# Natural row order for the first four token tiles of a fused layer-norm, linear-attention and gated-MLP kernel

## The chip, the cores and the metric

The kernel runs on one core of one Trainium2 chip. Times are device microseconds (us) of that core; a shorter time is better. Before the change the median of the first three runs was 213.92 us (213.84 to 214.03). Runs of one kernel usually agree within 0.3%.

## The reference, cut to what matters

```python
xn = layernorm(x)                       # x: 2048 tokens x 512, bf16
qkv = xn @ wqkv                         # 32 heads of 16
# feature maps softmax(+-q w_phi), softmax(+-k w_phi); linear attention; @ wo
# gated MLP: ((xn @ w_gate) * (xn @ w_up)) @ w_down, inner width 1792
out = x + attention(xn) + mlp(xn)
```

Every token is treated alike. Which token sits in which partition of which tile is free, as long as loads, residual loads and stores agree.

## The kernel before

The 2048 tokens are 16 tiles of 128 (partition x 512 features). One helper maps a tile to rows of DRAM, for the loads of `x`, for the second (residual) loads of `x` and for the stores:

```python
def rows(ap, t0, n):
    g, r = divmod(t0, 4)
    return ap[g * 512:(g + 1) * 512, :].rearrange("(p r) d -> p r d", r=4)[:, r:r + n, :]
```

So tile 0 holds rows 0, 4, 8, ... of the first 512. A row is 1 KB, and the rows of one tile lie 4 KB apart. Tiles 0 and 1 are loaded in halves of 256 columns, from two queues, so that the layer norm can start early:

```python
for t in range(2):
    load_x_half(t, 0, SP)      # 64 KB: 128 pieces of 512 B
    load_x_half(t, 1, ACT)
load_x(2, 1)                   # 128 KB: 128 rows of 1 KB
load_v(ACT, 1)                 # v weights, 128 KB each
load_v(SP, 0)
load_v(ACT, 3)
load_v(SP, 2)
load_x(3, 1)
load_gu(SP, 0, (0,))           # first gate weights
load_gu(SP, 0, (1,))           # first up weights
...
```

The head of the compute, in an order that is fixed on each engine:

```python
warm(7)                          # matmuls of 512 columns on constants
warm(1, 512, [("x", 0)])         # one more when tile 0 is there
ln_mean_split(0)                 # half the mean on VectorE, half on ScalarE
ln_mean_split(1)
ln_center_split(0)               # VectorE
ln_center_split(1)
x_transpose(0, 2, 0)             # TensorE, then ScalarE copies from PSUM
ln_mean_split(2)                 # waits for tile 2
x_transpose(0, 3, 1)
warm(1, 128)
x_transpose(1, 4, 0, DVE)        # copied from PSUM by VectorE, behind tile 2's mean
ln_center_whole(2)
x_transpose(1, 5, 1, DVE)
warm(1, 128)
... # v matmuls of tiles 0 and 1 (weights 1, 0), tile 2's transposes, v matmuls (3, 2), ...
... # v of tile 2, first gate half, tile 3's transposes, first up half, ...
```

Of the kernel before, what the change touches and what calls it, by code (L numbers as in the profile page):

```python
# [125 lines left out]
def _build(nc, es, A_x, A_wqkv, A_w_phi, A_wo, B_w_gate, B_w_up, B_w_down, out):  # L126
# [137 lines left out]

    def rows(ap, t0, n):
        g, r = divmod(t0, 4)
        return ap[g * 512:(g + 1) * 512, :].rearrange("(p r) d -> p r d", r=4)[:, r:r + n, :]

    def load_x(t0, n, eng=SP):
        o = sb("x", t0 * 512, n * 512).rearrange("p (t d) -> p t d", t=n)  # L270
        i = rows(x_flat, t0, n)
        sc.dma(eng, lambda e: e.dma_start(o, i), [], [("x", t) for t in range(t0, t0 + n)], n * 131072)

    def load_x_half(t, h, eng):
        c = slice(h * 256, h * 256 + 256)
        o, i = x_tile(t)[:, c], rows(x_flat, t, 1)[:, 0, c]
        sc.dma(eng, lambda e: e.dma_start(o, i), [], [("x", t) if h else ("x", t, 0)], 65536)  # L277
# [4 lines left out]
    def load_residual(t0):  # L282
        o = sb("xr", (t0 % 4) * 512, 1024).rearrange("p (t d) -> p t d", t=2)
        i = rows(x_flat, t0, 2)
        over = [("ek", 2 + t0 // 2, h) for h in range(2)] if t0 < 4 else []
        sc.dma(SP, lambda e: e.dma_start(o, i), [], [("xr", t % 4) for t in (t0, t0 + 1)] + over, 262144)
# [1119 lines left out]
```

## Time and profile before

| what | value | where |
|---|---|---|
| time, median of the first 3 runs | 213.92 us | times |
| span of the profiled run | 212.2 us | page |
| TensorE (PE) busy | 208.5 us, 98% | page |
| loads of 64 KB, issue to landing | 2.5 us (SP), 2.7 us (ACT) | DMA view |

Lines of the page of the kernel before: the span, the busy row of the engines, DMA packets, and the chain that ended last by engine (shares of the span).

```profile
span 212.2 us, 4050 instructions
PE 208.5 (98%) x1476; PEld 125.2 (59%) x1476; DVE 166.0 (78%) x281; ACT 144.7 (68%) x350; POOL 108.7 (51%) x137
DMA packets 49539, 22.29 MB, mean 105 GB/s; under 512 B 38128, under 2 KB 47984, under 8 KB 49520
PE 97%; DMA 1%; DVE 1%; SPq 0%; issue 0%
```

From the DMA view of the kernel before, the half loads of tiles 0 and 1 on SP (how many, KB each, median us from issue to landing):

```profile
arena<-in_A_x_dram SPq DMA_DIRECT2D x2, 64.0 KB, 2.5
```

PE has work almost from end to end. A change of the loads of `x` can only matter before PE's unbroken stretch starts. That head is in the timeline; columns are start, length, engine, line, operation, tiles, shape, count, and in brackets the idle time before with its releaser. First VectorE (DVE) of the kernel before:

```profile
3.30 0.42 DVE L436 TENSOR_SCALAR_CACHE_REDUCE arena<-arena 128x256 bf16<-128x256 bf16 x1 [3.30 <-DMA arena<-in_A_x_dram]
3.81 0.42 DVE L436 TENSOR_SCALAR_CACHE_REDUCE arena<-arena 128x256 bf16<-128x256 bf16 x1
4.15 1.11 DVE L443 TENSOR_SCALAR arena<-arena 128x256 bf16<-128x256 bf16 x4
5.27 0.42 DVE L436 TENSOR_SCALAR_CACHE_REDUCE arena<-arena 128x256 bf16<-128x256 bf16 x1
5.62 0.29 DVE L492 COPY arena<-ps 128x256 bf16<-128x256 bf16 x1
```

The first line waits 3.30 us for tile 0. The second is tile 1's mean, then come four centerings, then tile 2's mean, and only behind it the copy that PE wants. PE in the same stretch:

```profile
4.55 0.54 PE L483 MATMUL ps<-arena 128*128 128x128 bf16 x4 [0.16 <-DVE arena L443]
5.56 1.23 PE L247 MATMUL ps<-arena 128*128 128x512 bf16 x4
```

PE waits 0.16 us for the first centering and then transposes (L483). The four v matmuls (L247) start at 5.56, and from 5.96 on PE doesn't stop. Three lines of the chain in order of time (start, length, what) say why PE started at 4.55: a load of `x` ended at 3.78, and VectorE's mean and centering lie between the two.

```profile
1.24 2.54 DMA arena<-in_A_x_dram
4.55 0.54 PE ps L483 x4
5.96 0.82 PE ps L247 x3
```

### The profile page before, as it was taken

What the parts mean: (1) busy time and instruction counts of PE and PEld (TensorE: products, weight loads), DVE (VectorE), ACT (ScalarE), POOL (GpSimd) and SP (SyncE); (2) the same over time, 40 slices, a digit from 0 to 9 for tenths busy, and PEclk for the clock granted to TensorE, in tenths of its full rate; (3) what the DMA queues carried; (4) which work ended last, traced back from release to release, by engine and by line L of the source; (5) the groups of instructions that cost most, each with busy time, mean ns of one, the idle gap of its engine ahead of it and who ended that gap; (6) DMA issues with size and microseconds to landing.
All of it is one profiled execution on the core that took longest, in us unless ns stands there. A gap on an engine that the chain in (4) does not pass through costs nothing.

```text
span 212.2 us, 4050 instructions
## 1 busy us (share of the span) xinstructions
PE 208.5 (98%) x1476; PEld 125.2 (59%) x1476; DVE 166.0 (78%) x281; ACT 144.7 (68%) x350; POOL 108.7 (51%) x137
## 2 busy tenths in 40 slices
PE   8999999999999999999999999999999999999995
PEld 2664444444554444444444444556888898899884
DVE  3687699998996647659889989896888898897622
ACT  5469998886989999978878977564534444432220
POOL 4030483343311448998895482104658649558540
PEclk9999999999999999999999999999999999999999
DMA  5999228479400220331421223413276726556411
GB/s 158 307 271 371 87 50 174 101 210 311 99 3 0 49 49 3 69 60 24 81 51 19 55 47 49 108 56 62 49 78 134 187 47 159 125 129 147 124 49 49
DMA packets 49539, 22.29 MB, mean 105 GB/s; under 512 B 38128, under 2 KB 47984, under 8 KB 49520
## 3 DMA queue, kind: packets, MB, share of 16 engines
q1 hardware_dynamic: 48944, 21.65, 43.5%
q10 hardware_dynamic: 576, 0.39, 0.6%
q8 instruction: 11, 0.18, 0.4%
q14 instruction: 8, 0.07, 0.1%
HBM read 11.03 MB, written 2.10 MB: 62 GB/s over the span
## 4 chain that ended last, share of the span: by engine, by line
PE 97%; DMA 1%; DVE 1%; SPq 0%; issue 0%
PE ps L247 91%; PE ps L562 2%; PE ps L620 2%; DMA arena<-in_A_x_dram 1%; PE ps L390 1%; PE ps L483 1%; DVE arena L933 0%; SPq L277 0%; DVE arena L436 0%; DVE arena L443 0%; PE ps L1010 0%
## 5 line engine op out<-in xcount | busy, mean ns | idle before, releaser
L247 PE MATMUL ps<-arena 128*128 128x512 bf16 (+2 forms) x1160 | 199.9, 330 | 0.0
L247 PEld LDWEIGHTS ps<-arena 128*128 128x128 bf16 (+1 forms) x1160 | 110.7, 98 | 73.5 <-DVE arena L492 0.3
L228 ACT ACTIVATE arena<-ps 128x512 bf16<-128x512 f32 (+3 forms) x117 | 59.2, 537 | 17.5 <-PE ps L247 12.4
L228 ACT ACTIVATE arena<-arena 128x32 f32<-128x32 f32 (+8 forms) x131 | 52.4, 424 | 5.8 <-DVE arena L903 3.0
L903 DVE TENSOR_TENSOR arena<-ps,arena 128x512 f16<-128x512 f32 (+1 forms) x56 | 38.4, 686 | 19.0 <-ACT arena L228 13.6
L525 POOL TENSOR_TENSOR arena<-arena 128x1024 bf16<-128x1024 bf16 x16 | 30.9, 1933 | 38.1 <-ACT arena L228 38.1
L228 ACT ACTIVATE arena<-ps,arena 128x512 bf16<-128x512 f32 (+1 forms) x55 | 35.5, 670 | 10.1 <-PE ps L247 10.0
L515 DVE TENSOR_REDUCE arena<-arena 128x64 f32<-128x1024 bf16 x32 | 38.6, 1211 | 3.4 <-ACT arena L228 3.4
L864 POOL TENSOR_TENSOR arena<-arena 128x256 f16<-128x256 f16 x32 | 24.2, 768 | 13.0 <-DMA arena<-arena 11.7
L228 ACT ACTIVATE ps<-ps 128x256 f32<-128x256 f32 x24 | 8.8, 368 | 29.0 <-PE ps L247 29.0
L842 DVE TENSOR_TENSOR arena<-arena 128x896 f16<-128x896 f16 x32 | 23.8, 750 | 3.2 <-PE ps L247 3.1
L933 DVE SCALAR_TENSOR_TENSOR arena<-ps,arena 128x256 bf16<-128x256 f32 (+1 forms) x24 | 13.5, 570 | 10.4 <-PE ps L247 10.0
L782 POOL TENSOR_TENSOR arena<-arena 128x512 f16<-128x512 bf16 x14 | 16.2, 1173 | 4.7 <-DVE arena L903 3.3
L968 POOL TENSOR_TENSOR arena<-arena 128x512 f32<-128x512 f32 x8 | 9.5, 1191 | 17.2 <-ACT arena L228 17.2
L531 POOL TENSOR_TENSOR arena<-arena 128x512 bf16<-128x512 bf16 x16 | 17.1, 1071 | 0.9
L630 DVE TENSOR_TENSOR arena<-ps,arena 128x512 f16<-128x512 f32 x16 | 11.0, 689 | 1.4
L414 DVE BATCH_NORM_STATS2 arena<-arena 128x6 f32<-128x512 bf16 x16 | 10.4, 673 | 0.2 <-DMA arena<-in_A_x_dram 0.2
L529 POOL TENSOR_TENSOR arena<-arena 128x32 f32<-128x32 f32 x16 | 4.2, 264 | 9.5 <-ACT arena L228 9.5
L677 DVE BATCH_NORM_STATS2 arena<-arena 128x6 f32<-128x512 bf16 x14 | 9.0, 681 | 0.0
L562 PEld LDWEIGHTS ps<-arena 128*128 128x128 bf16 x128 | 6.1, 97 | 3.5
L811 DVE TENSOR_TENSOR arena<-arena 128x1792 f16<-128x1792 f16 (+1 forms) x8 | 7.0, 904 | 0.0
L620 PEld LDWEIGHTS ps<-arena 128*128 128x128 bf16 x128 | 6.2, 97 | 1.2
(54 smaller groups left out, 67.6 us busy)
## 6 DMA issues: line engine op xcount, KB each, us to landing
arena<-in_A_x_dram SPq DMA_DIRECT2D x8, 256.0 KB, 3.3
out_dram<-arena SPq DMA_DIRECT2D x15, 128.0 KB, 2.0
arena<-in_B_w_down_dram SPq DMA_DIRECT2D x1, 1792.0 KB, 8.1
arena<-in_A_x_dram SPq DMA_DIRECT2D x3, 512.0 KB, 4.2
arena<-arena SPq DMA_TRANSPOSE x44, 3.0
arena<-in_B_w_gate_dram SPq DMA_DIRECT2D x1, 640.0 KB, 8.8
arena<-in_B_w_up_dram SPq DMA_DIRECT2D x1, 640.0 KB, 10.0
arena<-in_B_w_gate_dram SPq DMA_DIRECT2D x1, 512.0 KB, 5.1
```

The costliest lines, as they stand in the source:

```text
L228: return sc.step(ACT, lambda e: e.activation(out=out_ap, in_=in_ap, func=func, scale=scale, **kw), reads, writes, 130.0 + 0.833 * n)
L247: ins = e.matmul(out_ap, lhsT=l, rhs=r, start=start and i == 0, stop=stop and i == npair - 1, **kw)
L515: dve(lambda e: e.tensor_reduce(out=sm, in_=e_v, axis=AX.X, op=ALU.add), [(name, s, 0), (name, s, 1)], [("sums", sr)], 1024)
L525: pool(lambda e: e.tensor_tensor(out=e_w, in0=e_w, in1=r_w, op=ALU.mult), [(name, s, 0), (name, s, 1), ("rs", n)], [(name, s, 0), (name, s ...
L531: pool(lambda e: e.tensor_tensor(out=e_v[:, :, 1, :], in0=e_v[:, :, 1, :], in1=rat[:, :, None].to_broadcast([128, H, 16]), op=ALU.mult), [ ...
L620: ins = e.matmul(bank(b0 + c // 4, (c % 4) * CW, CW), lhsT=ph[:, c, :], rhs=kvz_v[:, c, :], start=True, stop=True)
L630: dve(lambda e: e.tensor_tensor(out=o_tile(t).rearrange("p (b h f) -> p b h f", b=2, f=16), in0=nd[:, :, :, 0:16], in1=w_v[:, r].unsqueeze ...
L782: pool(lambda e, ft=ft: e.tensor_tensor(out=hH_v[:, ft, 0:512], in0=hT_v[:, ft, 0:512], in1=r2w, op=ALU.mult), [("hT", ft, 0), "r2w", ("x" ...
L842: dve(lambda e, k=k, i0=i0, i1=i1, op=op: e.tensor_tensor(out=s_block(p, k), in0=i0, in1=i1, op=op), ks + more, [s_key(p, k)] + over.get(k ...
L864: pool(lambda e, k=k, i0=i0, i1=i1, op=op: e.tensor_tensor(out=so_block(p, k), in0=i0, in1=i1, op=op), ks + [("so", p, m) for m in more], ...
L903: dve(lambda e: e.tensor_tensor(out=h_v[:, ft, sg * 512:(sg + 1) * 512], in0=bank(bu), in1=g, op=ALU.mult), [("ps", bu), ("g", s)] + ([("j ...
L933: dve(lambda e: e.scalar_tensor_tensor(out=o, in0=src, scalar=inv, in1=resid, op0=ALU.mult, op1=ALU.add), keys + [rkey, "inv"], [("ostg", ...
```

## The change

The rows of tiles 0 to 3 are taken in natural order: tile 0 has rows 0 to 127, tile 1 rows 128 to 255, and so on. The intent is that each of their loads reads one contiguous block of DRAM. (The half loads of tiles 0 and 1 read half of every row, so theirs is a block with gaps: 512 B out of each 1 KB.)

```diff
     def rows(ap, t0, n):
         g, r = divmod(t0, 4)
+        if g == 0:
+            return ap[t0 * 128:(t0 + n) * 128, :].rearrange("(r p) d -> p r d", r=n)
         return ap[g * 512:(g + 1) * 512, :].rearrange("(p r) d -> p r d", r=4)[:, r:r + n, :]
```

## The prediction

> **What bounds the kernel.** TensorE. The page gives PE 208.5 us busy of a 212.2 us span (98%) at full granted clock; the chain that ended last is 97% PE, 1% DMA (loads of x) and 1% DVE. From 5.96 us on the chain is back-to-back matmuls until the last eviction at 209.59 us. So x's loads can only matter in the first 6 us.
>
> **The head, from the timeline and the records of landings.** Loads of 64 KB (halves of tiles 0 and 1) are issued from 0.79 us and land after a median 2.5 us (SP) and 2.7 us (ACT). The first half of tile 0 lands at 3.28 us (its mean starts at 3.30), that of tile 1 at 3.79; the chain holds 2.54 us of DMA ending there. Then VectorE's means and centerings, with PE starting transposes at 4.55 after waiting 0.16 us. Tile 2 (128 KB, issued 1.70) has its last landing at 5.26, and its means on ACT and DVE both start at 5.27: they seem to wait for it by about 0.1 us, and behind it on DVE is the copy from PSUM (5.62, 0.29 us) for which PE waits until 5.96. Tile 3 lands at 7.18, but PE reaches its transposes only at 9.01, busy all the while.
>
> **What the change does.** The tokens of a 512-row group are permuted among tiles 0 to 3. Instructions, shapes and their order stay. A row stays 1 KB per partition (512 B in a half load), so packets keep number and size in these six loads; only the pitch of DRAM rows falls from 4 KB to 1 KB. (A half load still reads half of every row.) Against it, the two residual loads of tiles 0 to 3 (256 KB, issued about 135.6 us) had 2 KB runs and get twice as many of 1 KB; their data is wanted only after 147 us. Stores keep 1 KB rows.
>
> **Cost.** Packets of 512 B take some 27 ns each, so moving bytes is not what makes 2.5 us; most is latency. The Trainium skill, "DMA: Bandwidth & Descriptors", section Latency and other measured facts, reports slow DRAM row pitches from 2 MiB up (207 GB/s at 512 KiB); 4 KB is far below, and I expect no such effect. What I see for a gain: the last of 16 engines lands 1.13 us after the median one in tile 2's load, against 0.5 to 0.8 us for the v weights (128 KB, pitch 3 KB). If that tail is due to the pitch, tile 2 comes 0.3 to 0.5 us earlier; about 0.1 us of it is on the critical path. Tiles 0 and 1 might gain 0 to 0.2 us. The v weights (landing 5.43, used 5.56; 5.92, used 6.19) cap the shift near 0.3 us. Expected gain: about 0.1 us of 213.9, under 0.1%.
>
> **Prediction.** 213.8 us, 8 times in 10 between 213.2 and 214.3. Faster by over 2%: 0.005; within 2%: 0.985; slower by over 2%: 0.01.
>
> **What would show it.** Tile 0's first mean at 3.2 to 3.4 us; tile 2's at 5.0 to 5.3; PE's unbroken stretch starting between 5.7 and 6.0; everything after shifted by that alone; PE busy 208.5; packets up by about 256 (of 49,539), all from the residual loads.
>
> **What would make it wrong.** The contiguous DRAM side of tiles 2 and 3 lowered to another split over the DMA engines (few engines would cost several us; fewer, larger reads would gain some tenths); tiles 0 and 1[...] landing later, moving the whole head; residual loads with more packets delaying the DMA transposes near 136 us enough to stall PE.

## The result

The changed kernel took 213.96 us (median of 6 runs, 213.73 to 214.26) against 213.90 us of the kernel before (6 runs, 213.84 to 214.26). The ratio is 1.0001, with a 95% interval of 0.9988 to 1.0013: the same. A ratio is the mean time of one kernel's fast runs over that of the other's of the same rounds, so not quite the ratio of the medians.

The page of the changed kernel, the same lines:

```profile
span 212.1 us, 4029 instructions
PE 207.6 (98%) x1455; PEld 125.9 (59%) x1476; DVE 166.1 (78%) x281; ACT 144.7 (68%) x350; POOL 108.9 (51%) x137
DMA packets 49795, 22.29 MB, mean 105 GB/s; under 512 B 38128, under 2 KB 48496, under 8 KB 49776
PE 95%; ACT 3%; issue 1%; DVE 0%
```

The same line of the DMA view, of the changed kernel:

```profile
arena<-in_A_x_dram SPq DMA_DIRECT2D x2, 64.0 KB, 2.0
```

PE shows 1455 matmuls instead of 1476 because 21 records are missing in this trace; weight loads still count 1476. The 256 additional packets are those of the residual loads. And the half loads land 0.5 us sooner, which is far more than was predicted. VectorE takes it up at once:

```profile
2.79 0.42 DVE L438 TENSOR_SCALAR_CACHE_REDUCE arena<-arena 128x256 bf16<-128x256 bf16 x1 [2.79 <-DMA arena<-in_A_x_dram]
3.21 0.42 DVE L438 TENSOR_SCALAR_CACHE_REDUCE arena<-arena 128x256 bf16<-128x256 bf16 x1
3.66 1.11 DVE L445 TENSOR_SCALAR arena<-arena 128x256 bf16<-128x256 bf16 x4
5.05 0.42 DVE L438 TENSOR_SCALAR_CACHE_REDUCE arena<-arena 128x256 bf16<-128x256 bf16 x1 [0.27 <-DMA arena<-in_A_x_dram]
5.39 0.29 DVE L494 COPY arena<-ps 128x256 bf16<-128x256 bf16 x1
```

The centerings start at 3.66 instead of 4.15. But then VectorE now waits 0.27 us for tile 2, and the copy comes at 5.39 instead of 5.62: of 0.5 us there are 0.23 us left. PE's chain has no wait for `x` any more:

```profile
0.82 3.57 PE ps L1012 x8
4.39 0.43 PE ps L485 x4
5.46 1.24 PE ps L247 x4
```

The chain puts the first transposes behind the end of the eighth warm-up matmul, at 4.39. Ends of matmuls are modelled, though, and by its own record the first transpose was issued earlier. PE's timeline of the changed kernel, the same lines as before the change:

```profile
4.19 0.63 PE L485 MATMUL ps<-arena 128*128 128x128 bf16 x4
5.37 1.33 PE L247 MATMUL ps<-arena 128*128 128x512 bf16 x4
```

So the first transpose starts 0.36 us earlier (4.19 against 4.55). The semaphore of the first centering came 0.48 us earlier (4.02 against 4.50), so the warm-up hid only about 0.12 us of it. The rest was lost step by step. The transposes start 107 ns apart, which is half the speed of those later in the trace. The first v matmul starts 0.18 us earlier than before, and the last semaphore that it waited for is that of its weights, which landed at 5.24. The second is 0.21 us earlier and the third 0.08 us (6.11 against 6.19), because TensorE still ran at half clock: by the spacing of the matmuls it sped up only between 5.76 and 6.11, while full clock is on record from 4.27 in the trace before. The span shrank by 0.1 us. The question is thus which of these losses are the rule, and whether the remaining 0.1 us is real.

### The profile page after: what moved, and what is told of

Read it like the earlier page. It is cut to its first block, busy times and chain, and to the rows that moved or that the text cites. A ratio compares the mean times of both kernels' runs of the same rounds, so it can differ in the third digit from the quotient of the medians.

```text
span 212.1 us, 4029 instructions
## 1 busy us (share of the span) xinstructions
PE 207.6 (98%) x1455; PEld 125.9 (59%) x1476; DVE 166.1 (78%) x281; ACT 144.7 (68%) x350; POOL 108.9 (51%) x137
## 2 busy tenths in 40 slices
DMA packets 49795, 22.29 MB, mean 105 GB/s; under 512 B 38128, under 2 KB 48496, under 8 KB 49776
## 4 chain that ended last, share of the span: by engine, by line
PE 95%; ACT 3%; issue 1%; DVE 0%
PE ps L247 88%; ACT arena L228 3%; PE ps L622 2%; PE ps L564 2%; PE ps L1012 2%; PE ps L392 1%; PE ps L485 1%; DVE arena L935 0%
## 5 line engine op out<-in xcount | busy, mean ns | idle before, releaser
L247 PE MATMUL ps<-arena 128*128 128x512 bf16 (+2 forms) x1139 | 197.9, 329 | 1.1
```

Of the source, the lines that this page charges most:

```text
L247: ins = e.matmul(out_ap, lhsT=l, rhs=r, start=start and i == 0, stop=stop and i == npair - 1, **kw)
```

## The experiments

Three things are read from each trace: when the last of the 16 DMA engines landed its part of a load (from the records of landings); when the third v matmul started (in the trace before it is the first that has no wait ahead of it, as PE doesn't stop from the second on, at 5.96); and when full clock was granted to TensorE (the trace's clock records, which are missing in three traces). The "first weight fold" is the start of the first matmul of `w_fold` (L390 of the kernel before), which multiplies the q or k weights by `w_phi`; it comes behind the head. All times are from the span's start.

| trace | row pitch | tile 0, first half landed | tile 1, first half landed | full clock from | third v matmul | first weight fold | span |
|---|---|---|---|---|---|---|---|
| before | 4 KB | 3.28 | 3.78 | 4.27 | 6.19 | 14.88 | 212.17 |
| rep_before | 4 KB | 3.26 | 3.81 | 5.02 | 6.11 | 14.80 | 212.10 |
| after | 1 KB | 2.77 | 3.18 | no record | 6.11 | 14.79 | 212.09 |
| rep_after | 1 KB | 2.69 | 3.98 | 5.82 | 6.33 | 15.02 | 212.31 |
| rep_after2 | 1 KB | 2.84 | 3.46 | 3.91 | 5.76 | 14.69 | 211.98 |
| pitch2 | 2 KB | 2.97 | 3.45 | 4.42 | 6.02 | 14.71 | 212.00 |
| pitch16 | 16 KB | 3.08 | 3.92 | 4.89 | 6.23 | 14.91 | 212.16 |
| free01 | 4 KB | 3.27 (not waited for) | 3.82 (not waited for) | no record | 6.11 | 15.05 | 212.33 |
| nat_warm5 | 1 KB | 2.86 | 3.32 | no record | 6.12 | 15.20 | 212.50 |
| nat_tuned | 1 KB | 2.93 | 3.30 | 8.51 | 6.15 | 16.00 | 213.29 |
| old_tuned | 4 KB | 3.25 | 4.03 | 10.50 | 6.73 | 17.28 | 214.58 |
| nat_order7 | 1 KB | 2.71 | 3.85 | 4.63 | 6.03 | 15.47 | 212.77 |
| old_order7 | 4 KB | 3.27 | 3.93 | 4.46 | 6.11 | 15.19 | 212.48 |
| nat_g1first | 1 KB | 2.83 | 3.39 | 5.55 | 5.84 | 15.48 | 212.77 |

The theories are: **A**, the 4 KB pitch makes loads land late, and the gain of the change is hidden by PE's warm-up, by tile 2 and by the weights. **B**, the earlier landing was chance. **C**, the moment when TensorE gets full clock differs from run to run and swamps what is left. **D**, the doubled packets of the residual loads cost it back. Later came **E**, that the head waits for tiles 0 and 1 alone, and **F**, that an edit in the order was itself harmful.

### Replicas, and other row pitches

`rep_before` and `rep_after` are the two kernels unchanged.

> The kernel before, unchanged, for a second trace. If the 4 KB row pitch causes the late landings (theory A), the first 64 KB half load of tile 0 again lands its last engine 0.4 to 0.6 us after the median engine (0.51 in the first trace) and tile 1's first half near 3.8 us. If the difference between the two first traces was chance (rival B), the tail can come out anywhere from 0.1 to 0.5 us. The moment at which TensorE goes from about 107 ns to about 56 ns per 128-column matmul may differ from the first trace (before 4.55 us there) if it is a matter of chance.

> The changed kernel, unchanged, timed in five rounds and traced again. Theory A: last landings of the four half loads again within 0.15 us of the median engine, tile 0's first mean at 2.7 to 2.9 us. Rival B (chance): tails up to 0.5 us. Time: ratio 0.999 to 1.000 to the kernel before. If the TensorE clock ramp is chance and ate the gain in the first trace (theory C), its end may now come before 5 us and the span be up to 0.3 us shorter than 212.1; if it is not chance, it comes between 5.4 and 6.1 us again.

`pitch2` spreads tiles 0 and 1 over the first 256 rows and tiles 2 and 3 over the next:

```diff
+        if g == 0:
+            return ap[t0 // 2 * 256:(t0 // 2 + 1) * 256, :].rearrange("(p r) d -> p r d", r=2)[:, t0 % 2:t0 % 2 + n, :]
```

> Rows at a pitch of 2 KB: tiles 0 and 1 share the first 256 rows, tiles 2 and 3 the next 256. The residual loads keep their 2 KB runs, so packets stay 49,539. Theory A (pitch): tails of the half loads between those of 4 KB and of 1 KB, or like 1 KB; first mean at 2.8 to 3.1 us. Rival B: no relation to the pitch. Rival D (the doubled packets of the residual loads cost the changed kernel something): this one would be faster than the changed kernel by 0.05 us or more with the same head; otherwise the same within 0.1 us. Ratio 0.998 to 1.001.

`pitch16` interleaves all tiles over all rows:

```diff
-        g, r = divmod(t0, 4)
-        return ap[g * 512:(g + 1) * 512, :].rearrange("(p r) d -> p r d", r=4)[:, r:r + n, :]
+        return ap.rearrange("(p r) d -> p r d", r=16)[:, t0:t0 + n, :]
```

> All sixteen tiles interleaved over all 2048 rows, so rows lie at a pitch of 16 KB in the head's loads. Theory A (pitch): tails as with 4 KB or longer, 0.5 to 1.0 us for the half loads, first mean at 3.3 us or later, time up by 0 to 0.6 us. Rival B: as with any other. Everything after the head should only shift.

**Measured.** `rep_before` took 213.85 us (one run, state unknown). `rep_after` took 214.11 us (ratio 1.001, 0.9998 to 1.0022), `pitch2` 213.85 us (0.9996, 0.9982 to 1.0011), `pitch16` 214.31 us (1.0015, 1.0001 to 1.0029; if anything slower, though its trace has the span of the kernel before, 212.2 us).

The landing of the *first* half load is not chance. The five traces with a 4 KB pitch have it at 3.25 to 3.28 us, the seven with natural order at 2.69 to 2.93. Its sixteen landings in the trace before are a staircase from 2.51 to 3.28 us; in the trace after, all lie between 2.48 and 2.77. So B falls for this load. But "the longer the pitch, the later" isn't what the runs show either: 16 KB gave 3.08 us, earlier than 4 KB, in its one trace. So the order of the rows makes the difference, and why isn't shown.

For the second load B is partly right. Tile 1's first half landed at 3.18 to 3.98 us with natural order; in `rep_after` it was 0.92 us behind its own median engine. Then PE starts its transposes even later than in the trace before, as the chain of `rep_after` shows:

```profile
1.24 2.74 DMA arena<-in_A_x_dram
4.75 0.65 PE ps L485 x4
6.00 0.93 PE ps L247 x4
```

The table also settles D. From the first weight fold to the end of the span it takes 197.25 to 197.30 us in all fourteen traces, with doubled residual packets (`after`: 212.086 - 14.794 = 197.29) and without (`before`: 212.171 - 14.876 = 197.30; `pitch2`: 212.004 - 14.706 = 197.30). Every difference of time between traces arose before that fold, which starts between 14.7 and 17.3 us. And in six of them (before, rep_before, after, rep_after, pitch2, pitch16) the stretch from the third v matmul to the fold is 8.69 us each time: there the first 6 us decided.

### What is all of tiles 0 and 1 worth?

In `free01` (rows at 4 KB) the layer norm of tiles 0 and 1 reads a constant tile, so nothing waits for their loads. Its output is wrong, which doesn't matter for the time.

```diff
+    pool(lambda e: e.memset(sb("fake", 0, 512), 0.5), [], ["fake"], 512)
-        act(xn_tile(t)[:, 256:], x_tile(t)[:, 256:], [("x", t)], ...
+        act(xn_tile(t)[:, 256:], src01(t)[:, 256:], [key01(t)], ...      # "fake" if t < 2; likewise mean and centering on VectorE
-    warm(1, 512, [("x", 0)])
+    warm(1, 512, ["fake"])
```

> The kernel before, but the layer norm of tiles 0 and 1 reads a constant tile instead of the loaded one, so that no wait for these four loads is left (the result is wrong on purpose; the loads still run). It shows all that earlier landings of tiles 0 and 1 can be worth. Theory A (eight warm-up matmuls hold TensorE until 4.39 us, then tile 2's load and the v weights): first transposes at 4.2 to 4.5 us, the third matmul with v weights at 5.9 to 6.1 us against 6.19 and 6.11 in the two traces of before, span 211.9 to 212.1, so 0.1 to 0.3 us gained at most. Rival E (the head waits for tiles 0 and 1 alone): third matmul before 5.6 us and span below 211.6.

**Measured.** 213.94 us, ratio 1.0001 (0.9988 to 1.0014): no gain that four runs could show by taking the wait away altogether; the interval leaves room for about 0.25 us. The PE timeline of this run:

```profile
4.19 0.63 PE L491 MATMUL ps<-arena 128*128 128x128 bf16 x4
4.62 0.31 PE L1018 MATMUL ps<-const-bfloat16-1.0 128*128 128x128 bf16 x1
5.28 1.68 PE L248 MATMUL ps<-arena 128*128 128x512 bf16 x4
```

PE started its transposes as soon as the warm-up let it, with no wait. Up to 5.15 us PE's records are those of `after` within 2 ns: there, too, nothing of PE's wait for `x` was left. As in `after`, the first v matmul (5.28) came when its weights had landed (5.14). In this run the v matmuls start 0.43 us apart (5.28, 5.68, 6.11, 6.54), which is the slow clock, against 0.22 us in fast stretches. So the 0.3 us by which the first v matmul was earlier than in the trace before were spent in running at half speed; and from the third v matmul to the fold it took 8.94 us instead of 8.69, so the span (212.33) is even longer. E is refuted: it wanted spans below 211.6, and the four runs have 212.0 to 212.4. For C this is one trace.

### Taking the hiding waits away: a failed repair

Three edits should expose the gain: (1) five warm-up matmuls instead of seven; (2) tile 2's mean behind the copies of tiles 0 and 1; (3) tile 2's load behind the first v weights. `nat_warm5` is the changed kernel with (1); `nat_tuned` has all three with natural rows, `old_tuned` all three with the old rows.

```diff
-    warm(7)
+    warm(5)
```
```diff
     x_transpose(0, 2, 0)
-    ln_mean_split(2)
     x_transpose(0, 3, 1)
     warm(1, 128)
     x_transpose(1, 4, 0, DVE)
-    ln_center_whole(2)
     x_transpose(1, 5, 1, DVE)
+    ln_mean_split(2)
+    ln_center_whole(2)
```
```diff
-    load_x(2, 1)
     load_v(ACT, 1)
     load_v(SP, 0)
+    load_x(2, 1)
```

> The changed kernel with five instead of seven warm-up matmuls before the one that waits for x, so that TensorE is free from about 3.4 us. Theory A, first half (the warm-up hides the earlier landing): first transposes at 3.9 to 4.1 us if tile 1 lands without a straggler, but the third v matmul still at 5.7 to 6.1 us, because the copy for tile 1 stands behind tile 2's mean; a gain of 0 to 0.2 us. If the warm-up were not what hides it, transposes start as before at 4.2 to 4.8 us. Clock ramp: fewer busy microseconds ahead of it, so it may end later.

> The changed kernel with five warm-up matmuls, with the means of tile 2 moved behind the copies of tiles 0 and 1 on VectorE and ScalarE, and tile 2's load issued after the first v weights. Theory A: with the three waits that hide it gone, the natural order gains: v matmuls start at 4.9 to 5.3 us and the third at 5.3 to 5.7 us, span 211.4 to 211.8, ratio to before 0.997 to 0.999. Rival B (landing by chance): no gain over the same head with the old rows, within 0.1 us.

> The kernel before (rows at a pitch of 4 KB) with the same three edits of the head. Theory A: transposes wait for the late landings, so the third v matmul comes 0.2 to 0.5 us later than with the natural order under the same head: 5.7 to 6.1 us, span 211.8 to 212.1, ratio 0.998 to 1.000. Rival B: the same as with the natural order, within 0.1 us.

**Measured.** `nat_warm5` 214.06 us (1.001, 0.9994 to 1.0025). Its first transpose started at 4.11 us, only 0.08 us before that of `after`, and now waited for the centering: the warm-up had hidden little. `nat_tuned` 215.04 us (1.0042, 1.0025 to 1.0058) and `old_tuned` 215.52 us (1.0077, 1.0056 to 1.0097): both clearly slower than the kernel before, and the expectations of both missed. The chain of `nat_tuned`:

```profile
4.22 0.65 PE ps L485 x4
5.50 1.71 PE ps L247 x4
7.64 2.65 PE ps L247 x12
```

Four v matmuls take 1.71 us, 0.43 each. Full clock was granted only at 8.51 us here and at 10.50 us in `old_tuned`; with seven warm-ups and a clock record it came between 3.91 and 5.82. In these two traces the full-clock stretch is 204.800 us long; in the others with a record it is 208.213 us. The two differ by 3.413 us, and they are 60 and 61 times 3.413 us. The clock is thus switched at steps of 3.41 us. The Trainium skill, "TensorE: Matmul & The Clock Gate", Part 1, describes this: TensorE runs at half clock until a busy window of some 3.4 us has gone by, and the windows run freely, so their phase differs from run to run. The traces agree with it: the 3.41 us step, 427 ns against 216 ns per 512-column matmul, and a grant anywhere between 3.91 and 5.82 us for kernels with seven warm-ups. With two warm-ups fewer PE stood idle ahead of the transposes (0.43 us in `nat_tuned`; 0.35 and 0.73 us in `old_tuned`, by the timeline's waits), and the clock came later. That the idle time delayed it is likely but not shown: `nat_warm5` also had 0.42 us, and its matmuls were fast from about 6.5 us on.

The two `tuned` kernels differ by their rows alone and come out at 1.0042 and 1.0077, with intervals that just overlap. The start of their transposes shows in one trace each what the rows did: 4.22 us with natural rows, 4.80 us with the old ones. But full clock also came 2 us later in the old one, and whether by chance or by the longer idle time isn't known, so how much of the difference in time is the rows' own stays open.

### The same order with all warm-ups

`nat_order7` and `old_order7` keep edits (2) and (3) and go back to seven warm-ups. `rep_after2` is the changed kernel a third time.

```diff
-    warm(5)
+    warm(7)
```

> Natural rows, tile 2's means behind the copies and its load behind the first v weights, but with all seven warm-up matmuls, so that TensorE has no idle gap before 4.39 us. Theory C (what made the kernels with five warm-ups slower is that TensorE reached full clock one window later): full clock is granted by 4.2 to 6.5 us again, no transpose before 4.39, span 211.8 to 212.2, ratio 0.998 to 1.000, some 1 us faster than with five warm-ups. Rival F (the new order of loads or of VectorE's work made them slower): still over 214.5 us.

> The same head with the old rows at a pitch of 4 KB. Theory A and C: transposes at 4.5 to 4.8 us, so at most 0.2 to 0.4 us later than with natural rows; ratio 0.999 to 1.001; difference to the natural order at most 0.3 us. Rival F: still over 215 us.

> The changed kernel a third time, for a larger sample. Theory A and C: tile 0's first half lands at 2.65 to 2.95 us again; the time from the first weight fold of TensorE to the end is 197.25 to 197.31 us as in every trace so far; full clock granted anywhere from 4.2 to 6.5 us; ratio to before 0.9995 to 1.0015.

**Measured.** `nat_order7` 214.52 us (1.0018, 1.0005 to 1.0031), `old_order7` 214.21 us (1.0008, 0.9996 to 1.002), `rep_after2` 214.16 us (1.0006, 0.9992 to 1.0021). Full clock came at 4.63 and 4.46 us again, and compared with their five-warm-up twins the medians fell by 0.5 us (natural) and 1.3 us (old), with the kernel before at 213.92 us in both sets of rounds. That is theory C's part of the failed repair, smaller than expected for the natural rows. The expected ratios of 1 or less were missed, though, and rival F is right in part: `nat_order7` is slower than the kernel before (F had said over 214.5 us), while `old_order7` is not told apart from it (F had said over 215 us). In the trace of `nat_order7`, moving tile 2 back made PE wait for tile 2's centering:

```profile
6.84 0.40 PE L485 MATMUL ps<-arena 128*128 128x128 bf16 x4 [0.21 <-DVE arena L450]
```

With this order the natural rows weren't faster than the old; their median was 0.3 us worse. The natural trace had a late engine in tile 1 (3.85 us, hardly before the 3.93 us of the old rows) and late up weights (9.76 us), for which PE waited.

`rep_after2` is the lucky run of the changed kernel: full clock at 3.91 us, tile 1 at 3.46, third v matmul at 5.76, which is 0.35 to 0.43 us ahead of the two traces of before. Yet its span is only 0.12 to 0.19 us shorter. The weight-load line of PE says where the rest went:

```profile
9.03 0.77 PEld L247 LDWEIGHTS ps<-arena 128*128 128x128 bf16 x8 [0.24 <-DMA arena<-in_B_w_up_dram]
```

PE was early enough to run into the next load, the first up weights, which landed at 8.99 us. They land behind everything issued before them, and the change moves them little (8.87 and 9.08 us in the two traces of before; 8.72, 9.20 and 8.99 in the three of after).

### The last wait

`nat_g1first` is the changed kernel with the second gate tile's first half ahead of the first up tile's, so that the up weights are wanted 0.44 us later.

```diff
     u0a()
-    g1a()
+    # (g1a() now stands ahead of u0a())
```

> The changed kernel with one swap in TensorE's order: the second gate tile's first half ahead of the first up tile's first half, so that the up weights, for which TensorE waited 0.24 us in the third trace of the changed kernel, are wanted 0.44 us later. Theory (each wait behind the loads of x takes the gain in turn; the up weights are the last of them): no wait for the up weights; from the third v matmul to the first weight fold 8.68 to 8.70 us also when the third v matmul starts before 5.9 us; ratio 0.998 to 1.0005. If the head is lucky (full clock before 5 us, no late engine in tile 1) the span is 211.7 to 211.9. Rival: something else caps the head at a span of 212.0.

**Measured.** 214.09 us, ratio 1.0000 (0.9980 to 1.0019). The trace is an unlucky one and doesn't answer the question: the *gate* weights had a late engine (9.11 us instead of 7.69 to 7.92 in the traces of after), and PE waited for them:

```profile
9.16 0.61 PE L247 MATMUL ps<-arena 128*128 128x256 bf16 x4 [0.78 <-DMA arena<-in_B_w_gate_dram]
```

That is more than the whole gain of the head. Up to there this trace is a fourth one of the changed kernel's head, and an early one: its third v matmul started at 5.84 us although full clock came only at 5.55. Against `after` that is 0.27 us, 0.12 of it because the first v weights landed earlier (5.00 against 5.24) and 0.15 because the clock did come earlier than there. So in two of four heads with natural rows (5.76 and 5.84, against 6.11 and 6.33) PE came to this point 0.27 to 0.43 us earlier than in the two traces of before, and both times a wait for gate or up weights took most or all of it back. No version was found that is clear of noise faster than the kernel before; `pitch2`, at 0.9996, comes nearest and is not told apart from it.

### All timed runs together

The 18 runs of the changed kernel have a median of 214.07 us and a mean of 214.12; the 52 runs of the kernel before have 213.91 and 214.01. The means differ by 0.11 us, with a 95% margin of about 0.16 (from both spreads). So what is left is at most a loss of a few tenths of a microsecond, and nothing shows a gain. Six of the 18 and nine of the 52 are over 214.2 us. Late clock and late engines produce such runs in the traces; which of them it was in the untraced runs isn't known. Whether natural rows make the weights' late engines likelier stays open: the up weights landed at 9.5 us or later in three of seven traces with natural rows and in none of five with the old ones, which is too few to tell, and some of these traces have other edits too.

## Why the prediction was right or wrong, point by point

- **The time was right**: 213.8 us predicted, range 213.2 to 214.3, measured 213.96; "within 2%" held. That tests little, as the kernel before (213.90) lies in the same range. A gain of 0.1 us was forecast. Against the two traces of before, the first of after has a span shorter by 0.01 and 0.08 us, the second one longer by 0.14 and 0.21, the third one shorter by 0.12 and 0.19; so the size of the gain is not confirmed.
- **TensorE bounds the kernel and only the head can change: right.** The 197.3 us behind the first weight fold are equal in all fourteen traces.
- **"tiles 0 and 1 might gain 0 to 0.2 us" failed.** It is the mis-sized term: tile 0's first half came 0.32 to 0.59 us earlier in the natural-order traces than in those at 4 KB, and its mean began at 2.79 us, outside the stated 3.2 to 3.4. The step behind it, "4 KB is far below, and I expect no such effect", was an inference from the row pitches in the Trainium skill, "DMA: Bandwidth & Descriptors", Latency and other measured facts, whose list starts at 512 KiB; the measurement decides against it.
- **Tile 2 "0.3 to 0.5 us earlier": at best the low end.** It landed at 5.25 and 5.09 us in the traces of before, at 5.02, 4.74 and 4.81 in those of after, 0.31 us earlier in the mean. With the other traces that load it at the same place (`free01` 4.93; `nat_warm5` 4.98, `nat_g1first` 4.69) it is 0.24. The reading that VectorE waits for it was right; with the change it waits visibly (0.27 us).
- **The cap of "near 0.3 us" was about right, its cause right in part.** The prediction named the v weights. They are one of the caps: the last semaphore of the first v matmul was theirs in `before` (landed 5.42, started 5.56), in `after` (5.24, 5.37) and in `free01` (5.14, 5.28). But they landed earlier than the prediction took for granted, and in `rep_after2` the third v matmul came 0.35 to 0.43 us earlier. It also had the copy that waits behind tile 2's mean. It did not have the other caps: the warm-up, which let the first transpose start at 4.19 and no sooner (0.36 us earlier than before); the half clock; and in the two early heads the gate or up weights.
- **PE's unbroken stretch between 5.7 and 6.0: right by its timing in the first trace** (second v matmul at 5.76, 5.96 before), not in `rep_after` (6.11) or `rep_after2` (5.53). "Everything after shifted by that alone" failed in `rep_after2`, where PE ran into the wait for the up weights.
- **Packets up by 256, from the residual loads, at no cost: right** (49,795 against 49,539; the tail of the span unchanged).
- **Missed altogether: the clock's phase.** Full clock was granted anywhere from 3.91 to 5.82 us in kernels with seven warm-ups and a record, and by the spacing of the matmuls still later in two without one (`after` between 5.76 and 6.11, `free01` after 6.5). Where it is late, PE runs what it got earlier at half speed; in `free01` the third v matmul was in the end no earlier than in the second trace of before (6.11 us). A late clock doesn't decide alone: `nat_g1first` got it at 5.55 us and had the second-earliest third v matmul.

## What to carry to other kernels

Before speeding up a load, look at what its consumer's consumer is doing at that moment: here VectorE got its data 0.5 us sooner, TensorE's first transpose came 0.36 us sooner, and the third v matmul 0.08 us sooner in one trace, 0.43 at best and later than before in another. Behind the wait that was shortened stood others of the same size (the v weights; VectorE's 0.27 us for tile 2; the up weights, 0.24 us). Don't shorten a warm-up to collect such a gain without looking at when full clock is granted; with two matmuls fewer it came at 8.51 and 10.50 us in two of three traces, against 5.82 at the latest on record with seven (after 6.5 in `free01`, by the matmuls' spacing). And where a head of 6 us depends on a free-running clock window and on the last of 16 engines, take several traces before explaining a tenth of a microsecond.

## What the Trainium skill lacked or had wrong

- "DMA: Bandwidth & Descriptors", Latency and other measured facts, lists DRAM row pitches from 512 KiB up. Here a small one mattered for a 64 KB load of 512 B pieces: last engine at 3.25 to 3.28 us with rows 4 KB apart, 2.69 to 2.93 us with 1 KB, one trace each 2.97 us with 2 KB and 3.08 us with 16 KB. The cause isn't known.
- The same page gives a fixed cost and a mean, but no figure for how far the last of the 16 engines of one DMA lags behind the others. Here the last engine of a load of 64 to 256 KB was 0.1 to 2 us behind the median one (tile 0: 0.10 us in the trace after, 0.51 us before; gate weights in `nat_g1first`: 9.11 against 7.10 us), and it is the last one that the wait ends with.
- "TensorE: Matmul & The Clock Gate", Part 1, fits: steps of 3.41 us, and a phase that differs from run to run. It doesn't say how much idle time a window bears. Here full clock was granted at 3.91 us in `rep_after2`, only 3.09 us after its first matmul (0.82), so not all of a 3.41 us window has to be busy. And with 0.42 to 0.43 us idle between warm-up and transposes, one kernel was granted it at 8.51 us while the matmuls of another were fast from about 6.5 us.
